# Attention, a max-of-three layer and a leaky layer in split fp32: plain-fp32 pairs, a longer result ring, and Strassen operands made on VectorE alone

## The chip, the cores and the metric

One core of a Trainium2 chip. The metric is the device time of one execution in microseconds (us), lower is better. The engines are named as in the profile: PE (TensorE's matmuls), PEld (its weight loads), DVE (VectorE), ACT (ScalarE), POOL (GpSimd), SP (SyncE, which only issues transfers here).

## What is computed

```python
def _attn_ref(q, k, v, w_phi):            # 4 batches, 8 heads, 576 positions, 64 wide
    def phi(x):
        proj = np.einsum('bhsd,df->bhsf', x, w_phi)          # 128 features
        proj = proj - np.max(np.abs(proj), axis=-1, keepdims=True)
        return np.concatenate([np.exp(proj), np.exp(-proj)], axis=-1)
    q_p, k_p = phi(q), phi(k)
    kv = np.einsum('bhsf,bhsd->bhfd', k_p, v)
    z = np.sum(k_p, axis=2)
    num = np.einsum('bhsf,bhfd->bhsd', q_p, kv)
    den = np.einsum('bhsf,bhf->bhs', q_p, z)[..., None] + 1e-06
    return num / den

def _moe_ref(x, w1, w2, w3, w_out):       # 2304 tokens, 512 -> 768 -> 512
    h = np.maximum(np.maximum(x @ w1, x @ w2), x @ w3)
    return h @ w_out

def _moe2_ref(x, w_in, w_out, alpha):     # 512 -> 2048 -> 512
    h = x @ w_in
    g = np.maximum(h, 0.0) + alpha * np.minimum(h, 0.0)
    return g @ w_out
```

The attention's result goes through the first of the two dense pairs and then through the second. The first pair's weights and the second's come as 64-bit floats and are brought to 32 bits on the chip.

## The kernel before

**Numbers.** Most products are made of split operands: an fp32 tile is written as a high part of type `fp32r` (`hi_act` on ACT or `hi_dve` on DVE) and the rest (`sub`, high part taken from the tile), and a product is three matmuls, high times high, high times low and low times high (`three`). A *plain* product is one matmul of fp32 tiles; the trace records each of those as two instructions.

**The five stages.** (1) Attention, in 16 pairs of heads (`pairs`, 4 per batch). `keys(pair)` projects the keys, takes the largest magnitude of each row, makes both exponentials on ACT and adds keys times values up in one PSUM bank (`kvp`); `queries(pair)` does the same for the queries with a transpose in between, then the numerator and denominator (`num`). The queries of a pair run beside the keys of the next one, at a lower priority. (2) Layer 1 (`layer1`): three products of the attention's result with `w1`, `w2`, `w3` and their maximum, 48 units, of which those of a batch can run once all four pairs of that batch have their result `x`. They fill PE while the later pairs are worked on. (3) Layer 2, `w_out`: 8 chunks of 288 tokens, each with 6 operands `hr` loaded and split by `load_h`, four products, and the results `yo` copied out of PSUM by ACT and stored from ACT's queue. (4) Layer 3, `w_in` with the leaky step. (5) The last layer, by Strassen's scheme: 9 blocks of 256 tokens, each in two halves of the inner dimension; a half has seven products, taken in the order `ORDER = (0, 5, 6, 4, 1, 3, 2)`, each of 12 matmuls. The seven operands `o` of a half are made by `left(block, half)`: two loads `a` (512 KB each), four sums `s1` to `s4` on DVE, and for each operand a high part on ACT and a rest on DVE or POOL. The operands of half 1 have seven places of their own (`op4`); those of half 0 share `ring2`'s 18 places with 14 tiles of the right-hand operand, which stay, so four places turn over.

**Order.** The program is written for a scheduler that puts every engine's instructions in one fixed sequence, by priorities (`tc.high_priority`) and a model of times. Each engine then works its sequence strictly in order: an instruction that waits holds up all that stand behind it on that engine. A tile of a pool can be written again when the last reader of the tile that had its place is done.

**What the change and the steps touch.** `plain` (L146) and `plain_kv` (L149) say which pairs use plain products: batch 0 for the projections, batches 0 and 1 for keys times values; `load_pair`, `features`, `exp_keys` (L206), `keys`, `queries` (L295) follow them. `CONVERT_IN` (L38, L416) says after which pairs the three weight tiles `w123t` of one column block are brought to 32 bits and split: after pairs 0 and 2 to 6. `load_h` (L492) and the loop of layer 2 (L524) hold the buffers of `hr` and `yo`. `left` (L558) makes the last layer's operands.

```python
            for a in range(4):                                       # exp_keys, L215
                A.activation(ev[:, a, 0], pv[:, a], AF.Exp, bias=mx[:, a : a + 1])
                A.activation(ev[:, a, 1], pv[:, a], AF.Exp, bias=my[:, a : a + 1], scale=-1.0)
...
            sub(G if n % 2 and block + half else V, ov[:, 1], src, ov[:, 0])   # left, L578
```

Of the kernel before, what the change touches and what calls it, by code (L numbers as in the profile page):

```python
# [10 lines left out]
F32 = mybir.dt.float32  # L11
# [23 lines left out]
EPS = 1e-6  # L35
XBUFS = (6, 6)
LAG = 1
CONVERT_IN = (0, 2, 3, 4, 5, 6)  # L38
SOON, NOW, LATER, LAST = 400, 1000, -100, -200


# [9 lines left out]
def tile_kernel(ctx: ExitStack, tc: tile.TileContext, qT, kT, tails, v, w_phi, w1, w2, w3, w_out, w_in, w_out2, alpha, out):  # L51
# [92 lines left out]
            raws[pair, what] = t  # L144

    def plain(pair):  # L146
        return pair[0] == 0

    def plain_kv(pair):  # L149
        return pair[0] < 2  # L150
# [55 lines left out]
    def exp_keys(pair):  # L206

        ops = features(pair, "k")
        for g, tiles in enumerate(GROUPS):
            pv, mx = project(ops, tiles)  # L210
            my = ap.tile([P, 4], F32, tag="my", bufs=4, name="my")
            V.tensor_scalar(my, mx, -1.0, None, op0=ALU.mult)
            e = ap.tile([P, 1024], F32, tag="e", bufs=2, name="ke")
            ev = e.rearrange("p (a s f) -> p a s f", s=2, f=P)
# [22 lines left out]
    def keys(pair):  # L237

        rv = raws[pair, "v"]
        if not plain_kv(pair):  # L240
            if not vs:
                vs.extend(ap.tile([P, 5, 3, D], F32R, tag=tag, bufs=1, name=tag) for tag in ("vh", "vl"))
                part = slice(None)
            else:
                part = slice(None, None, 2)
            vh, vl = vs
            hi_act(vh[:, :, part], rv[:, :, part])
            sub(V, vl[:, :, part], rv[:, :, part], vh[:, :, part])
        kvp = bank("kv", 1, "kvp")
        first = True  # L250
        for tiles, e in exp_keys(pair):
            n = len(tiles) * 512
            if plain_kv(pair):
                ops = ((rv, e),)
            else:
                kh = ap.tile([P, 1024], F32R, tag="kh", bufs=2, name="kh")
                kl = ap.tile([P, 1024], F32R, tag="kl", bufs=2, name="kl")
                hi_act(kh[:, :n], e[:, :n])
                sub(V, kl[:, :n], e[:, :n], kh[:, :n])
                ops = ((vh, kh), (vl, kh), (vh, kl))  # L260
            yield
            for i, t in enumerate(tiles):
                for h in range(2):
                    c = slice(i * 512 + h * 256, i * 512 + h * 256 + 256)
                    for x, y in ops:
                        nc.tensor.matmul(
                            kvp[:, h * 256 : h * 256 + 256],
                            x[:, t, h : h + 2].rearrange("p a d -> p (a d)"),
                            y[:, c],
                            start=first,  # L270
                            stop=t == 4 and y is ops[-1][1],
                            skip_group_check=True,
                        )
                        first = False
        yield
        kvs = ap.tile([P, 512], F32, tag="kvs", bufs=1, name="kvs")
        A.activation(kvs, kvp, AF.Copy)
        kvt = bank("kv", 1, "kvt")
        for i in range(4):
            nc.tensor.transpose(kvt[:, i * P : (i + 1) * P], kvs[:, i * P : (i + 1) * P], ident)  # L280
        if plain(pair):
            kvf = ap.tile([P, 2, 2, P], F32, tag=("kvh", "kvl")[pair[1] % 2], bufs=2, name="kvf")
            A.activation(kvf.rearrange("p a b c -> p (a b c)"), kvt, AF.Copy)
            kvs_of[pair] = (kvf,)
            return
# [8 lines left out]

    def queries(pair):  # L295

        parts = ("q",) if plain(pair) else ("qh", "ql")
        qf = []
        for n, (o, w) in enumerate(CHUNKS):
            qf.append([])  # L300
            for x in parts:
                tag = f"qh{n}" if x != "ql" and pair[1] % 2 * len(x) != 1 else f"ql{n}"
                qf[n].append(ap.tile([P, 2, 2, w], F32 if plain(pair) else F32R, tag=tag, bufs=1, name=x))
        nd = [ap.tile([P, S], F32, tag="nd", bufs=3, name="nd") for _ in range(2)]

        def num(n):
            o, w = CHUNKS[n]
            kv = kvs_of[pair]
            for h in range(2):
                pn = bank("p1", 3, "pn") if plain(pair) else bank("pn", 1, "pn")  # L310
                ops = []
                for s in range(2):
                    q_ = [t[:, h, s] for t in qf[n]]
# [7 lines left out]

        for g, tiles, pp in chain(project_queries(pair), tail()):
            o, w = (0, 2 * P, SM)[g], ST if g == 2 else 2 * P
            pt = bank("pt", 1, "pt")
            for i in range(len(tiles)):
                for h in range(2):
                    c = h * len(tiles) * P + i * P
                    nc.tensor.transpose(pt[:, c : c + P], pp[:, 2 * i + h], ident)
            n = min(g, 1)
            dst = [t[:, :, :, o - CHUNKS[n][0] : o - CHUNKS[n][0] + w] for t in qf[n]]  # L330
            if plain(pair):
                e = dst[0]
            else:
                e = ap.tile([P, 2, 2, 256], F32, tag="qe", bufs=2, name="qe")[:, :, :, :w]
            pv = pt[:, : 256 * len(tiles)].rearrange("p (h s) -> p h s", h=2)[:, :, -w:]
            A.activation(e[:, :, 0], pv, AF.Exp)
            A.activation(e[:, :, 1], pv, AF.Exp, scale=-1.0)
            if not plain(pair):
                (hi_dve if g == 1 else hi_act)(dst[0], e)
                sub(V, dst[1], e, dst[0])  # L340
            yield
# [64 lines left out]
    for i, pair in enumerate(pairs):  # L406
        if i + 1 < len(pairs):
            load_pair(pairs[i + 1])
        with tc.high_priority(offset=0 if plain(pair) else SOON if pair[0] == 1 else NOW):
            if pair == (1, 0):  # L410
                hi_dve(wph, wraw)
                sub(V, wpl, wraw, wph)
            run(*([at_priority(LATER, queries(last))] if last else []), keys(pair))
            last = pair
        if i in CONVERT_IN:
            with tc.high_priority(offset=LAST if i < NPAIR - 1 else 0):  # L416
                for j in range(3):
                    run(split_w123(len(w) - (j > 0), j))
        u0 = 3 * (i - NPAIR) - LAG
        for u in range(u0, u0 + 3):  # L420
            if u >= 0:
# [69 lines left out]

    def load_h(c, k):  # L492
        hh, hl = x_tiles(max(c % 2, k // XBUFS[0]))
        pool, tag, bufs = ((xp, "xr", 3), (xp, "xr", 3), (xp, "s1", 2), (gp, "neg", 2))[(2 * c + k) % 4]
        if c == 0:
            pool, tag, bufs = xp, "xr", 3
        hr = pool.tile([P, CH], F32, tag=tag, bufs=bufs, name="hr")
        nc.sync.dma_start(hr, h_d[k, :, c * CH : (c + 1) * CH])
        hi_act(hh, hr)
        sub(V, hl, hr, hh)  # L500
# [23 lines left out]
    for c in range(2 * B):  # L524
# [5 lines left out]
        for m in range(KT):  # L530
# [2 lines left out]
            for k in range(NF1):  # L533
                ops += three(wo[k][:, 0, ms], wo[k][:, 1, ms], *hs[c, k])
            products(p2[m][:, :CH], ops)
            yo = xp.tile([P, CH], F32, tag="ho", bufs=2, name="yo")
            A.activation(yo, p2[m][:, :CH], AF.Copy)
            nc.scalar.dma_start(y_d[m, :, t0 : t0 + CH], yo)
        convert(2)
# [18 lines left out]
    def left(block, half):  # L558

        ready[block, half] = res = {}  # L560
        a = []
        for kh in range(2):
            t = ap4.tile([P, 4, 2 * T], F32, tag="a", bufs=4, name="a")
            r = slice(kh * 8 + half * 4, kh * 8 + half * 4 + 4)
            nc.sync.dma_start(t, g_d[r, :, block * 2 * T : (block + 1) * 2 * T].rearrange("f p n -> p f n"))
            a.append(t)
        (a00, a10), (a01, a11) = ((t[:, :, :T], t[:, :, T:]) for t in a)
        s1, s2, s3, s4 = (ap4.tile([P, 4, T], F32, tag="s", bufs=4, name="s") for _ in range(4))
        V.tensor_tensor(s3, a00, a10, op=ALU.subtract)
        V.tensor_tensor(s1, a10, a11, op=ALU.add)  # L570
        V.tensor_tensor(s2, s1, a00, op=ALU.subtract)
        V.tensor_tensor(s4, a01, s2, op=ALU.subtract)  # L572
        for n, i in enumerate(ORDER):
            src = (a00, a01, s4, a11, s1, s2, s3)[i]
            o = op4.tile([P, 2, 512], F32R, name="o") if half else ring2.tile([P, 2, 512], F32R, tag="w", name="o")
            ov = o.rearrange("p a (f n) -> p a f n", f=4)
            hi_act(ov[:, 0], src)
            sub(G if n % 2 and block + half else V, ov[:, 1], src, ov[:, 0])  # L578
            res[i] = o
            yield  # L580

    V.tensor_scalar(al, al, -1.0, 1.0, op0=ALU.mult, op1=ALU.add)
    load_y(0, 0)
# [129 lines left out]
```

## Time and profile before

| what | value |
|---|---|
| runs of the kernel before | 941.51, 936.77, 939.18 us; median 939.18 |
| the profiled execution | 941.19 us, of which the span of the profile is 939.4 us |
| mean granted clock of TensorE | 0.989 of full speed |
| busy in the span | PE 906.3, DVE 658.9, ACT 487.0, POOL 155.1 us |
| attention beside the first units of layer 1 | about 0 to 377 us |
| layer 2, layer 3, last layer begin | about 466, 547, 750.5 us |

Busy times are shares of engine time; instructions of PE overlap, so the number of matmuls begun in a stretch tells more than its busy time. POOL's 155 us are the 51 rests of the last layer and the issuing of 140 stores.

### The profile page before, as it was taken

The page shows a single profiled execution, that of the slowest core. Times are in us where ns is not written, and L with a number is a line of the kernel's source. Part 1 is how long each engine was busy: PE and PEld are TensorE (multiplying, and loading weights), DVE is VectorE, ACT ScalarE, POOL GpSimd, SP SyncE. Part 2 cuts the span into 40 slices and gives each one's busy share as a digit, 9 for nine tenths or more (in the row PEclk, how much of TensorE's full clock was granted, in tenths as well). Part 3 has the DMA queues.
Part 4 walks back from the last instruction along what each step waited for, and adds up shares of the span by engine and source line. Part 5 has one row for each costly group of instructions (what it writes and reads, how often), then busy time and mean ns, then how long its engine had stood idle before and what let it go on. Part 6 is the DMA issues. An engine that isn't in the chain of part 4 may idle for free.

```text
span 939.4 us, 18181 instructions
## 1 busy us (share of the span) xinstructions
PE 906.3 (96%) x6730; PEld 881.6 (94%) x6730; DVE 658.9 (70%) x1281; ACT 487.0 (52%) x1148; POOL 155.1 (17%) x197
## 2 busy tenths in 40 slices
PE   8778899999999999999999999999999998999998
PEld 6556799999999999999999999999999998999998
DVE  5788866878888752689888575446544588878782
ACT  6667665867667841334356363335333354444441
POOL 0000000000000000001100013333333353444440
PEclk9998899999999999999999999999999999999999
DMA  8455422322233112566676755444643344444421
GB/s 275 142 160 158 131 66 58 101 90 85 79 87 86 33 40 57 190 180 189 198 222 219 246 168 159 152 145 156 206 146 116 113 124 116 154 139 131 135 70 45
DMA packets 83161, 126.01 MB, mean 134 GB/s; under 512 B 14208, under 2 KB 61952, under 8 KB 83072
## 3 DMA queue, kind: packets, MB, share of 16 engines
q1 hardware_dynamic: 71744, 99.47, 35.6%
q0 software_dynamic: 6720, 20.65, 6.1%
q10 hardware_dynamic: 4608, 4.72, 1.5%
q8 instruction: 53, 0.87, 0.4%
q14 instruction: 36, 0.29, 0.1%
HBM read 86.91 MB, written 35.46 MB: 130 GB/s over the span
## 4 chain that ended last, share of the span: by engine, by line
PE 39%; DVE 5%; DMA 5%; ACT 3%; issue 2%; ACTq 0%; DVEq 0%; SPq 0%
PE p L235 23%; PE acc L632 15%; DMA hr<-h_d 2%; DMA st<-in_w_in 2%; DVE o L73 1%; DMA y_d<-yo 1%; DMA st<-in_w_out 1%; ACT xh L67 1%; DVE xl L73 1%; ACT wt L80 1%; DVE s L572 0%; ACT o L67 0%; DVE wt L88 0%; ACT wq L67 0%; DVE wt L86 0%
## 5 line engine op out<-in xcount | busy, mean ns | idle before, releaser
L235 PE MATMUL p<-xh,w123t 128*128 128x288 f32 x1152 | 241.0, 298 | 1.1 <-DVE s L391 0.8
L235 PE MATMUL p<-xh,wi 128*128 128x288 f32 x1024 | 203.7, 296 | 0.0
L235 PEld LDWEIGHTS p<-xh,w123t 128*128 128x128 f32 x1152 | 187.0, 188 | 2.7 <-DVE s L391 1.3
L632 PE MATMUL acc<-wq,o 128*128 128x256 f32 x1512 | 181.7, 282 | 3.2 <-DVE o L73 2.9
L632 PEld LDWEIGHTS acc<-wq,o 128*128 128x128 f32 x1512 | 179.9, 190 | 4.9 <-DVE o L73 4.5
L235 PE MATMUL p<-xl,w123t 128*128 128x288 f32 x576 | 171.6, 298 | 0.0
L235 PEld LDWEIGHTS p<-xh,wi 128*128 128x128 f32 x1024 | 163.2, 188 | 0.0
L235 PE MATMUL p<-xl,wi 128*128 128x288 f32 x512 | 149.5, 293 | 0.0
L603 DVE SCALAR_TENSOR_TENSOR g<-neg,al,p 128x288 f32<-128x288 f32 x128 | 64.3, 512 | 63.6 <-ACT neg L601 59.9
L235 PEld LDWEIGHTS p<-xl,w123t 128*128 128x128 f32 x576 | 108.2, 188 | 0.3
L604 POOL DMA_DIRECT2D g_d<-g x128 | 69.5, 544 | 208.4 <-DVE g L603 204.7
L235 PEld LDWEIGHTS p<-xl,wi 128*128 128x128 f32 x512 | 97.1, 190 | 0.0
L601 ACT ACTIVATE neg<-p 128x288 f32<-128x288 f32 x128 | 51.0, 407 | 86.2 <-PE p L235 81.9
L395 POOL DMA_DIRECT2D h_d<-ho x12 | 7.3, 611 | 466.0 <-DVE ho L393 466.0
L235 PE MATMUL p<-xh,wo 128*128 128x288 f32 x384 | 77.3, 297 | 1.8 <-ACT xh L67 1.8
L67 ACT ACTIVATE o<-s 128x512 fp32r<-128x512 f32 x72 | 44.3, 629 | 54.3 <-PE acc L632 30.0
L73 DVE TENSOR_TENSOR xl<-xr,xh 128x288 fp32r<-128x288 f32 x96 | 42.2, 455 | 37.2 <-ACT xh L67 33.2
L67 ACT ACTIVATE xh<-xr 128x288 fp32r<-128x288 f32 x96 | 41.6, 449 | 47.4 <-DMA xr<-y_d 33.4
L235 PEld LDWEIGHTS p<-xh,wo 128*128 128x128 f32 x384 | 61.2, 188 | 2.5 <-ACT xh L67 2.5
L216 ACT ACTIVATE ke<-pj,mx 128x128 f32<-128x128 f32 x128 | 49.1, 384 | 21.9 <-DVE mx L193 21.6
L193 DVE TENSOR_REDUCE mx<-pj 128x4 f32<-128x512 f32 (+1 forms) x80 | 50.3, 632 | 14.4 <-PE pj L235 14.4
L73 POOL TENSOR_TENSOR o<-s,o 128x512 fp32r<-128x512 f32 x34 | 49.5, 1459 | 64.3 <-ACT o L67 59.4
(133 smaller groups left out, 1695.7 us busy)
## 6 DMA issues: line engine op xcount, KB each, us to landing
g_d<-g POOLq DMA_DIRECT2D x128, 144.0 KB, 2.2
a<-g_d SPq DMA_DIRECT2D x36, 512.0 KB, 3.8
st<-in_w_out SPq DMA_DIRECT2D x22, 512.0 KB, 4.1
wst<-in_w SPq DMA_DIRECT2D x18, 512.0 KB, 4.4
xr<-y_d SPq DMA_DIRECT2D x64, 144.0 KB, 2.4
st<-in_w_in SPq DMA_DIRECT2D x16, 512.0 KB, 3.9
v<-in_v SPq DMA_DIRECT2D x16, 480.0 KB, 3.8
hr<-h_d SPq DMA_DIRECT2D x48, 144.0 KB, 4.2
```

What stands on the lines that cost most here:

```text
L67: A.activation(dst, src, AF.Copy)
L73: eng.tensor_tensor(dst, src, hi.bitcast(F32), op=ALU.subtract)
L80: A.activation(w, high.bitcast(F32), AF.Abs)
L193: V.tensor_reduce(mx, pv, axis=AX.X, op=ALU.max, apply_absolute_value=True, negate=True)
L216: A.activation(ev[:, a, 0], pv[:, a], AF.Exp, bias=mx[:, a : a + 1])
L235: nc.tensor.matmul(dst, x, y, start=i == 0, stop=i == len(ops) - 1, **kw)
L395: (nc.gpsimd if b == B - 1 else nc.sync).dma_start(h_d[f, :, o : o + CH], ho)
L601: A.activation(neg, p, AF.Relu, scale=-1.0)
L603: V.scalar_tensor_tensor(g, neg, al[:, f : f + 1], p, op0=ALU.mult, op1=ALU.add)
L604: nc.gpsimd.dma_start(g_d[f, :, c * CH : (c + 1) * CH], g)
L632: nc.tensor.matmul(acc[i], x, y, start=half == 0 and f == 0 and n == 0 and PLACE[i][1] == 0, stop=half == 1 and f == 3 and n == 2, skip_gr ...
```

## The change

Five things are done at once.

1. `plain` now holds for the first five pairs (batch 0 and pair 0 of batch 1). In batch 1 the `kv` result, the queries' exponentials and `num` follow `plain_kv`, so they too are plain there. `num` of batch 1 takes its bank from `pn` (one) as before and that of batch 0 from `p1` (three); in batch 0 the second transposes of a pair's queries take `pn`'s bank and not `pt`'s.
2. In batch 0 the keys are treated as the queries are: DVE subtracts the largest magnitude into an SBUF tile `pp`, and ACT makes two exponentials of 512 columns out of it where it made eight of 128.
3. The 18 weight tiles `w123t` are converted 2, 1, 2, 1, 3, 3, 3, 3 at a time after pairs 0 to 7, where it was 3 after pairs 0 and 2 to 6.
4. In layer 2 the results `yo` alternate between two pools of two places (they had two in all), and `hr` has the three places of `xr` and the two of `s1` (it also had the two that `yo` now has).
5. In the last layer all rests are made on DVE, each sum is written next to the product that needs it first, and the two loads of a half share one tile of a pool of two where each had its own tile of a pool of four.

```diff
-CONVERT_IN = (0, 2, 3, 4, 5, 6)
+PLAIN = 5
+CONVERT_IN = (2, 1, 2, 1, 3, 3, 3, 3)
     def plain(pair):
-        return pair[0] == 0
+        return pair[0] * NPAIR + pair[1] < PLAIN
...
             pv, mx = project(ops, tiles)
+            e = ap.tile([P, 1024], F32, tag="e", bufs=2, name="ke")
+            ev = e.rearrange("p (a s f) -> p a s f", s=2, f=P)
+            if pair[0] == 0:
+                pp = ap.tile([P, 4, P], F32, tag="pp", bufs=2, name="pp")
+                less_max(pv, mx, pp)
+                A.activation(ev[:, :, 0], pp, AF.Exp)
+                A.activation(ev[:, :, 1], pp, AF.Exp, scale=-1.0)
+                yield tiles, e
+                continue
...
-        if plain(pair):
+        if plain_kv(pair):
             kvf = ap.tile([P, 2, 2, P], F32, tag=("kvh", "kvl")[pair[1] % 2], bufs=2, name="kvf")
...
-                pn = bank("p1", 3, "pn") if plain(pair) else bank("pn", 1, "pn")
+                pn = bank("p1", 3, "pn") if pair[0] == 0 else bank("pn", 1, "pn")
...
-            pt = bank("pt", 1, "pt")
+            pt = bank("pn" if pair[0] == 0 and g == 1 else "pt", 1, "pt")
...
-            if not plain(pair):
+            if not plain_kv(pair):
                 (hi_dve if g == 1 else hi_act)(dst[0], e)
                 sub(V, dst[1], e, dst[0])
...
-        if i in CONVERT_IN:
+        for _ in range(CONVERT_IN[i] if i < len(CONVERT_IN) else 0):
             with tc.high_priority(offset=LAST if i < NPAIR - 1 else 0):
-                for j in range(3):
-                    run(split_w123(len(w) - (j > 0), j))
+                n = sum(len(x) for x in w)
+                run(split_w123(n // 3, n % 3))
...
-        pool, tag, bufs = ((xp, "xr", 3), (xp, "xr", 3), (xp, "s1", 2), (gp, "neg", 2))[(2 * c + k) % 4]
-        if c == 0:
-            pool, tag, bufs = xp, "xr", 3
-        hr = pool.tile([P, CH], F32, tag=tag, bufs=bufs, name="hr")
+        tag, bufs = ("s1", 2) if c and k % 2 else ("xr", 3)
+        hr = xp.tile([P, CH], F32, tag=tag, bufs=bufs, name="hr")
...
-            yo = xp.tile([P, CH], F32, tag="ho", bufs=2, name="yo")
+            pool, tag = ((xp, "ho"), (gp, "neg"))[m % 2]
+            yo = pool.tile([P, CH], F32, tag=tag, bufs=2, name="yo")
...
-        a = []
+        a = ap4.tile([P, 2, 4, 2 * T], F32, tag="a", bufs=2, name="a")
         for kh in range(2):
-            t = ap4.tile([P, 4, 2 * T], F32, tag="a", bufs=4, name="a")
             r = slice(kh * 8 + half * 4, kh * 8 + half * 4 + 4)
-            nc.sync.dma_start(t, g_d[r, :, block * 2 * T : (block + 1) * 2 * T].rearrange("f p n -> p f n"))
-            a.append(t)
+            nc.sync.dma_start(a[:, kh], g_d[r, :, block * 2 * T : (block + 1) * 2 * T].rearrange("f p n -> p f n"))
...
-        V.tensor_tensor(s3, a00, a10, op=ALU.subtract)
-        V.tensor_tensor(s1, a10, a11, op=ALU.add)
-        V.tensor_tensor(s2, s1, a00, op=ALU.subtract)
-        V.tensor_tensor(s4, a01, s2, op=ALU.subtract)
-        for n, i in enumerate(ORDER):
-            src = (a00, a01, s4, a11, s1, s2, s3)[i]
+        def factor(i, src):
             o = op4.tile([P, 2, 512], F32R, name="o") if half else ring2.tile([P, 2, 512], F32R, tag="w", name="o")
             ov = o.rearrange("p a (f n) -> p a f n", f=4)
             hi_act(ov[:, 0], src)
-            sub(G if n % 2 and block + half else V, ov[:, 1], src, ov[:, 0])
+            sub(V, ov[:, 1], src, ov[:, 0])
             res[i] = o
-            yield
+
+        factor(0, a00)
+        V.tensor_tensor(s1, a10, a11, op=ALU.add)
+        V.tensor_tensor(s2, s1, a00, op=ALU.subtract)
+        yield
+        factor(5, s2)
+        V.tensor_tensor(s3, a00, a10, op=ALU.subtract)
+        yield
+        factor(6, s3)
+        yield
+        factor(4, s1)
+        yield
+        factor(1, a01)
+        yield
+        factor(3, a11)
+        V.tensor_tensor(s4, a01, s2, op=ALU.subtract)
+        yield
+        factor(2, s4)
```

**ACT's sequence at the first pair.** `ke` is the exponentials of one group of keys, `pj` the projections in PSUM, `mx` and `my` minus and plus the largest magnitude. Before:

```order
L216 ACTIVATE ke_120<-pj_113,mx_116 128x128
L217 ACTIVATE ke_120<-pj_113,my_118 128x128
L216 ACTIVATE ke_120<-pj_113,mx_116 128x128
L217 ACTIVATE ke_120<-pj_113,my_118 128x128
L216 ACTIVATE ke_120<-pj_113,mx_116 128x128
L217 ACTIVATE ke_120<-pj_113,my_118 128x128
L216 ACTIVATE ke_120<-pj_113,mx_116 128x128
L217 ACTIVATE ke_120<-pj_113,my_118 128x128
L216 ACTIVATE ke_140<-pj_133,mx_136 128x128
```

Now:

```order
L217 ACTIVATE ke_118<-pp_119 128x4x128
L218 ACTIVATE ke_118<-pp_119 128x4x128
L217 ACTIVATE ke_132<-pp_133 128x4x128
L218 ACTIVATE ke_132<-pp_133 128x4x128
L233 ACTIVATE ke_147<-ppt_141,signs_84 128x2x128 x2
```

Eight exponentials of a group have become two, and they read the SBUF tile `pp`, so the PSUM bank `pj` is free once DVE has made `pp`.

**DVE's sequence at the turn from one block of the last layer to the next.** Before, `o_10627` and `o_10633` are two of the last three rests of a block's half 0 (the one between them is on POOL), `s_10861` and `s_10863` are sums of its half 1, and `a_10992` is the first load of the next block's half 0:

```order
L644 TENSOR_TENSOR out0_10723<-acc_10485,u2_10721 128x256
L73 TENSOR_TENSOR o_10769<-s_10746,o_10769 128x512
L73 TENSOR_TENSOR o_10627<-a_10605,o_10627 128x512
L571 TENSOR_TENSOR s_10861<-s_10860,a_10856 128x512
L73 TENSOR_TENSOR o_10633<-s_10610,o_10633 128x512
L572 TENSOR_TENSOR s_10863<-a_10858,s_10861 128x512
L73 TENSOR_TENSOR o_10868<-a_10856,o_10868 128x512
L73 TENSOR_TENSOR o_10874<-s_10862,o_10874 128x512
L569 TENSOR_TENSOR s_10998<-a_10992 128x512
```

Now, with `o_10676`, `o_10679`, `o_10683` the last three rests of half 0 of the fifth block, `a_10654` its tile of loads and `a_10905` the sixth block's:

```order
L662 TENSOR_TENSOR out0_10773<-acc_10537,u2_10771 128x256
L74 TENSOR_TENSOR o_10818<-s_10795,o_10818 128x512
L74 TENSOR_TENSOR o_10676<-a_10654,o_10676 128x512
L74 TENSOR_TENSOR o_10679<-a_10654,o_10679 128x512
L583 TENSOR_TENSOR s_10908<-a_10905 128x512
L74 TENSOR_TENSOR o_10683<-s_10660,o_10683 128x512
L584 TENSOR_TENSOR s_10909<-s_10908,a_10905 128x512
L587 TENSOR_TENSOR s_10910<-a_10905 128x512
```

The next block's first sum `s_10908` now stands ahead of this block's last rest `o_10683`. It stands so at four turns, into the sixth, seventh, eighth and ninth block; at the earlier ones the last rest stands ahead of what reads the next load. The matmuls of these four blocks stand in the order of the products.

## Rows read from the trace of the kernel before

**Rows 1.** The page's part 1: busy time, share, instructions.

```profile
PE 906.3 (96%) x6730; PEld 881.6 (94%) x6730; DVE 658.9 (70%) x1281; ACT 487.0 (52%) x1148; POOL 155.1 (17%) x197
```

**Rows 2.** Windows of 25 us: length, busy time (instructions) by engine, granted clock, DMA.

```profile
75.00:100.00 25.00, 21.89 (x119) 19.07 (x117) 20.25 (x49) 19.82 (x52) 0.00 (x0) 0.86 0.50 145
...
125.00:150.00 25.00, 25.00 (x183) 24.47 (x182) 16.05 (x37) 13.88 (x38) 0.00 (x0) 1.00 0.20 57
```

**Rows 3.** PE's waits, whole span: us in total, times, longest.

```profile
PE pt L328 <- ACT q L337: 6.0, 3, 3.4
PE pj L235 <- ACT ke L217: 3.2, 2, 2.9
```

**Rows 4.** Groups by shape, 0 to 300 us: count, busy us, mean ns, idle before.

```profile
L336 ACT ACTIVATE qe<-pt 128x512 f32<-128x512 f32 x19 | 11.8, 623 | 3.1 <-PE pt L328 3.1
...
L197 DVE TENSOR_TENSOR pp<-pj,mx 128x512 f32<-128x512 f32 x28 | 19.1, 682 | 0.0
```

**Rows 5.** Timeline of ACT at the first keys: start, length.

```profile
7.15 0.36 ACT L217 ACTIVATE ke<-pj,my 128x128 f32<-128x128 f32 x1
7.40 0.37 ACT L216 ACTIVATE ke<-pj,mx 128x128 f32<-128x128 f32 x1
```

**Rows 6.** Timeline of PE: split and plain products back to back.

```profile
85.86 1.89 PE L235 MATMUL pn<-q,kvf 128*128 128x256 f32 x8
87.59 0.38 PE L328 MATMUL pt<-ident,ppt 128*128 128x128 f32 x2
...
155.08 0.28 PE L235 MATMUL pj<-wph,xhq 128*128 128x256 f32 x1
155.20 0.28 PE L235 MATMUL pj<-wpl,xhq 128*128 128x256 f32 x1
```

**Rows 7.** Windows in layer 2, and one at its end.

```profile
480.00:490.00 10.00, 9.09 (x67) 8.64 (x66) 7.86 (x17) 6.91 (x17) 0.00 (x0) 1.00 0.74 231
500.00:530.00 30.00, 28.06 (x203) 26.70 (x202) 24.26 (x51) 16.23 (x39) 0.00 (x0) 1.00 0.79 252
540.00:560.00 20.00, 20.00 (x154) 20.00 (x153) 15.20 (x34) 12.88 (x31) 3.24 (x5) 1.00 0.56 172
```

**Rows 8.** Waits of ACT, whole span.

```profile
ACT yo L537 <- DMA y_d<-yo: 15.9, 11, 4.3
...
ACT xh L67 <- DMA hr<-h_d: 10.2, 7, 3.0
```

**Rows 9.** Timeline of PE, start of the last layer.

```profile
750.50 27.26 PE L632 MATMUL acc<-wq,o 128*128 128x256 f32 x226
780.61 19.63 PE L632 MATMUL acc<-wq,o 128*128 128x256 f32 x152 [2.85 <-DVE o L73]
```

**Rows 10.** Timelines of DVE and POOL, start of the last layer.

```profile
755.99 1.38 DVE L73 TENSOR_TENSOR o<-s,o 128x512 fp32r<-128x512 f32 x1 [0.35 <-ACT o L67]
...
760.73 0.68 DVE L569 TENSOR_TENSOR s<-a 128x512 f32<-128x512 f32 x1
761.33 0.68 DVE L73 TENSOR_TENSOR o<-s,o 128x512 fp32r<-128x512 f32 x1
...
777.33 1.08 DVE L569 TENSOR_TENSOR s<-a 128x512 f32<-128x512 f32 x1
...
755.53 3.01 POOL L73 TENSOR_TENSOR o<-s,o 128x512 fp32r<-128x512 f32 x2 [3.04 <-ACT o L67]
```

**Rows 11.** Last layer: one window, ACT at a block's start, loads `a` issued and landed.

```profile
840.00:860.00 20.00, 19.96 (x170) 19.76 (x170) 16.43 (x24) 9.06 (x16) 9.27 (x7) 1.00 0.43 130
...
856.92 0.63 ACT L67 ACTIVATE o<-a 128x512 fp32r<-128x512 f32 x1 [0.83 <-PE acc L632]
858.35 0.63 ACT L67 ACTIVATE o<-a 128x512 fp32r<-128x512 f32 x1 [0.80 <-PE acc L632]
...
754.92 1.12 SPq L565 DMA_DIRECT2D a<-g_d  x2
...
DMA to landing us min/median/max: 3.7/3.8/5.0
```

More of the change, by code (lines that the diff above doesn't have):

```diff
@@ L210, in exp_keys @@
             pv, mx = project(ops, tiles)
+            e = ap.tile([P, 1024], F32, tag="e", bufs=2, name="ke")
[7 more added lines that the diff above has]
+                continue
             my = ap.tile([P, 4], F32, tag="my", bufs=4, name="my")
             V.tensor_scalar(my, mx, -1.0, None, op0=ALU.mult)
-            e = ap.tile([P, 1024], F32, tag="e", bufs=2, name="ke")
-            ev = e.rearrange("p (a s f) -> p a s f", s=2, f=P)
             for a in range(4):
@@ L295, in queries @@
     def queries(pair):
-        parts = ("q",) if plain(pair) else ("qh", "ql")
+        parts = ("q",) if plain_kv(pair) else ("qh", "ql")
         qf = []
@@ L302, in queries @@
                 tag = f"qh{n}" if x != "ql" and pair[1] % 2 * len(x) != 1 else f"ql{n}"
-                qf[n].append(ap.tile([P, 2, 2, w], F32 if plain(pair) else F32R, tag=tag, bufs=1, name=x))
+                qf[n].append(ap.tile([P, 2, 2, w], F32 if plain_kv(pair) else F32R, tag=tag, bufs=1, name=x))
         nd = [ap.tile([P, S], F32, tag="nd", bufs=3, name="nd") for _ in range(2)]
@@ L330, in queries @@
             dst = [t[:, :, :, o - CHUNKS[n][0] : o - CHUNKS[n][0] + w] for t in qf[n]]
-            if plain(pair):
+            if plain_kv(pair):
                 e = dst[0]
@@ L408, in tile_kernel @@
             load_pair(pairs[i + 1])
-        with tc.high_priority(offset=0 if plain(pair) else SOON if pair[0] == 1 else NOW):
-            if pair == (1, 0):
+        with tc.high_priority(offset=(0, SOON, NOW, NOW)[pair[0]]):
+            if i == PLAIN - 1:
                 hi_dve(wph, wraw)
@@ L560, in left @@
         ready[block, half] = res = {}
-        a = []
+        a = ap4.tile([P, 2, 4, 2 * T], F32, tag="a", bufs=2, name="a")
         for kh in range(2):
-            t = ap4.tile([P, 4, 2 * T], F32, tag="a", bufs=4, name="a")
             r = slice(kh * 8 + half * 4, kh * 8 + half * 4 + 4)
-            nc.sync.dma_start(t, g_d[r, :, block * 2 * T : (block + 1) * 2 * T].rearrange("f p n -> p f n"))
-            a.append(t)
-        (a00, a10), (a01, a11) = ((t[:, :, :T], t[:, :, T:]) for t in a)
+            nc.sync.dma_start(a[:, kh], g_d[r, :, block * 2 * T : (block + 1) * 2 * T].rearrange("f p n -> p f n"))
+        (a00, a10), (a01, a11) = ((a[:, kh, :, :T], a[:, kh, :, T:]) for kh in range(2))
         s1, s2, s3, s4 = (ap4.tile([P, 4, T], F32, tag="s", bufs=4, name="s") for _ in range(4))
-        V.tensor_tensor(s3, a00, a10, op=ALU.subtract)
-        V.tensor_tensor(s1, a10, a11, op=ALU.add)
-        V.tensor_tensor(s2, s1, a00, op=ALU.subtract)
-        V.tensor_tensor(s4, a01, s2, op=ALU.subtract)
-        for n, i in enumerate(ORDER):
-            src = (a00, a01, s4, a11, s1, s2, s3)[i]
+        def factor(i, src):
             o = op4.tile([P, 2, 512], F32R, name="o") if half else ring2.tile([P, 2, 512], F32R, tag="w", name="o")
```

## The prediction

> **What bounds the kernel now.** I read the page's busy times first, then windows along the span, PE's waits, and the timelines of the stages that the change touches. PE is busy for 96% of the span [rows 1], so the time is PE's work plus the stretches in which it starves, and a saving on another engine counts only there. In the windows, from 125 us on PE is busy in all of its 25 us with 183 matmuls; before that it is not: from 75 to 100 us it begins 119, is busy 21.9 of 25 us, and its granted clock averages 0.86, while DVE is busy 20.25 and ACT 19.8 us [rows 2]. So up to about 110 us DVE and ACT set the pace together, and after that PE does, except in two places. In layer 2, 67 matmuls begin from 480 to 490 us and 203 from 500 to 530 us, where an undisturbed window has 154 in 20 us, 0.130 us each [rows 7]: 10 and 28 too few, 4.9 us. At the start of the last layer PE stands for 2.85 us waiting for an operand's rest on DVE [rows 9]. From 840 to 860 us it starts 170 matmuls and is busy 19.96 of 20 us [rows 11]: there is nothing left to gain there, but something to lose.
>
> **Attention: what is taken off ACT.** In batch 0, 64 exponentials of 128 columns go, which start 0.25 us apart [rows 5], 16.0 us of ACT; 16 of 512 columns come, 0.62 us each [rows 4], 9.9 us: ACT is 6.1 us shorter. DVE gets 8 subtractions of 0.68 us [rows 4], 5.4 us; they lie on the same path, between projection and exponential. In PE's waits, 6.0 us go to transposes that wait for the bank `pt` until ACT has read it, and 3.2 us to projections that wait for a bank until ACT has made the exponentials out of it [rows 3]. The first gets a second bank; the second now waits for DVE's subtraction only. The gain lies between 0 (DVE, which gets more, sets the pace alone) and 9.2 us (both waits gone). I take 6 us, what ACT loses, since the bank that PE waits for is ACT's to give back. The splits that batch 1 drops on DVE and ACT I cost at nothing: they lie mostly after 110 us, where PE's own work covers them. Moving weight conversions to later pairs I cost at nothing too; they are fillers at a low priority, and the last of them, for the sixth column block, stands one pair later, ahead of the unit that needs it.
>
> **Attention: what PE pays.** Batch 1's products become plain: 27 projections (pair 0 of batch 1), 48 numerators of 256 and 48 of 320 columns go, as split matmuls; 9 plain projections and 16 and 16 plain numerators come. Split ones of 256 columns start 0.12 us apart; four plain ones (eight recorded) take 1.73 us, 0.43 each [rows 6]. By columns, 320 cost 0.15 and 0.54. Gone: 75 x 0.12 + 48 x 0.15 = 16.2; new: 25 x 0.43 + 16 x 0.54 = 19.4. PE gets 3.2 us more, and since this falls where it is full, all of it counts.
>
> **Layer 2.** ACT waits 15.9 us in 11 places for a `yo` to be stored before it can copy the next, and 10.2 us for `hr` [rows 8]. Behind a waiting copy stand the high parts of the next chunk, for which PE starves. Four places for `yo` remove the first wait; `hr` loses two places of seven, so late in a chunk its sixth load waits for the second to be split. The ends are 0 and the whole 4.9 us; I take 3.5, near the whole, since the removed wait is the larger one.
>
> **The start of the last layer.** DVE's operations with two SBUF inputs take 0.68 us undisturbed, and start 0.60 us apart; beside POOL's rests they take longer [rows 10]. Nine such, the first at 755.99 us with 1.38 and the last at 777.33 us with 1.08, take 13.9 us together (1.54 each) instead of 9 x 0.68 = 6.1: 7.8 us lost. POOL's nine rests of that stretch, about 1.5 us each there [rows 10], come to DVE at 0.60, 5.4 us. DVE is 2.4 us earlier, which takes that much off the 2.85 us. After the stop 152 matmuls take 19.63 us; at the 0.1206 us of the 226 before it (27.26 us) they would take 18.3 [rows 9], so the slower stretch after the stop costs 1.3 us, and goes with it. Together 3.7 us, between 0 and 4.15.
>
> **The running last layer.** In each block DVE now has 22 operations of 0.60 and 7 of half that width (0.34 us, an estimate from 0.68), 15.6 of the block's 19.8 us (168 matmuls at the pace of [rows 11]); this fits. What does not is a load that has come under a shared tile. Take a block's start as 0. Its fifth and sixth operands get their high parts on ACT at 1.4 and 2.85 us, when the first two products give their places back (856.92 and 858.35 us for a block that starts at 855.5) [rows 11]. The sixth's rest ends at 2.85 + 0.65 + 0.68 = 4.2 us, and it is the last reader of the tile `a`. Only then can both loads for the next block go out; before, each load had its own tile, and the first could go as soon as the sums were made. A load lands 3.8 us after its issue at the median and 5.0 at most; two issues that went out within 1.12 us of each other are among these [rows 11]. So the second lands at 8.4 to 9.6 us. In four blocks the next block's first sum, which reads both loads, stands in DVE's sequence ahead of the seventh operand's rest: this one is ready after 0.68 + 0.60 us, at 9.7 to 10.9. PE comes to the seventh product at 6 x 1.41 = 8.5 us and, after two matmuls on the high part, needs the rest at 8.7. It waits 1.0 to 2.2 us, four times. I take 1.6, the middle, as two loads together are nearer to the maximum but nothing else is on the queues: +6.4 us. If DVE also falls behind in the earlier blocks (15.6 us of work behind a load of 4.2 to 5.4 us is 19.8 to 21.0 for a block of 19.8, less one or two rests made meanwhile), the first of the four waits takes some 4 us more; the upper end is +11.
>
> The Trainium skill, DMA: Bandwidth & Descriptors, section Bandwidth, gives 6.15 us of transfer for 1 MB against the 3.8 us that the trace shows for one of these half-megabyte loads alone. As an estimate by that page, two loads together would land some 1.3 us later than I took, and the sum below would be 5 us higher; no run here has shown two issued back to back.
>
> **The sum.** -6 + 3.2 - 3.5 - 3.7 + 6.4 = -3.6 us. The profiled execution took 941.2 us, so 937.6 on its scale; it lies 2.0 us above the median of the runs, 939.2. Forecast for the median: **935.6 us**, 0.4% less. About 0.5%, 4.7 us, is what a measurement of this kernel can tell from no change.
>
> **Rivals** (all on the median's scale).
> - *The gains come whole and the loads come soon.* Both bank waits, all of layer 2's and the whole stop go, and PE waits 1.0 us in four blocks: -9.2 + 3.2 - 4.9 - 4.15 + 4.0 = -11.1, 928.1 us. For it: DVE keeps 19% of its time free before 110 us. Against: DVE's new work stands on the path. Chance 0.25.
> - *The last layer's loads decide, slower than before.* The first sum holds up the seventh rest for over 2 us, DVE drifts, and each stop lowers the clock as the one at 780 us did: +11 + 4 x 1.3 = +16.2 in place of +6.4, so +6.2, 945.4 us. It decides from a landing of about 5 us for the pair. For it: the maximum in the trace is from two loads near each other. Against: small stops in layer 2 left the granted clock at 1.00 [rows 7]. Chance 0.15.
> - *Attention gains nothing.* DVE sets the pace alone and PE still pays: +2.4, 941.6 us. For it: DVE is the busier of the two in the window [rows 2]. Chance 0.18.
> - *Layer 2 does not do what is said:* five places for `hr` starve PE as `yo` did: -0.1, 939.1 us. Chance 0.06.
>
> **How the numbers follow.** My sum has 0.36; its own range is 931 to 940, of which I give 0.16 to below 934.5 and 0.20 to above. Faster: 0.16 + 0.25 = 0.41. Slower: 0.15 + 0.02 from the upper side of the third rival. Same: 0.42. The range 926 to 946 takes in both outer cases and leaves out about 2 in 10 beyond them.
>
> **What would show it.** Right: in PE's waits the rows of `pt` and of `pj` behind ACT shrink; the row of `yo` behind its store goes; no stop near 778 us; and in blocks five to eight one wait each for DVE's `o`, 1 to 2 us, at the seventh product, with DVE idle until a load lands. Wrong: PE full through the last layer, matmuls from 25 to 110 us no denser than now, or ACT waiting for `hr` where it waited for `yo`.

## The result, and the profile after

The changed kernel takes **925.83 us** at the median of 6 runs (923.4 to 928.34), the kernel before 939.74 us in the same comparison: a ratio of 0.9855, 95% interval 0.9829 to 0.9882, 13.9 us less. The forecast was 935.6 us; the measured median lies 0.2 us under the range's lower end. The sign was right, the size was not: the sum had -3.6 us. The nearest case was the rival in which the gains come whole (928.1 us).

The changed kernel's profiled execution has a span of 926.4 us, 13.0 us under that of before (939.4). The page's part 1, which answers to [rows 1]:

```profile
PE 900.7 (97%) x6689; PEld 877.8 (95%) x6689; DVE 643.2 (69%) x1306; ACT 471.6 (51%) x1092; POOL 77.3 (8%) x146
```

The first matmul of each stage in the two timelines says where the 13.0 us are:

| stage | begins before, after | length before, after | difference |
|---|---|---|---|
| attention and layer 1, to layer 2's start | 0, 0 | 465.8, 462.1 | -3.7 |
| layer 2 | 465.8, 462.1 | 81.2, 78.0 | -3.2 |
| layer 3 | 547.0, 540.1 | 203.5, 204.4 | +0.9 |
| last layer, PE | 750.5, 744.5 | 184.9, 177.8 | -7.1 |

The prediction had -2.8, -3.5, 0 and +2.7 for these. The first three look well met, and the last is off by ten. The runs below show that the layer 2 row is not what it seems either. Nor is the whole first row the change's: runs 1 to 3 leave PE's, ACT's and DVE's sequences as they were up to layer 3, and in their traces layer 2 begins at 463.0, 463.4 and 464.0 us. Layer 3's 0.9 us was not looked into.

PE's timeline of the changed kernel's last layer is one row, where [rows 9] had two with a stop between them:

```profile
744.53 177.82 PE L650 MATMUL acc<-wq,o 128*128 128x256 f32 x1512
```

All 1512 matmuls follow one another at 0.1176 us. There is neither a stop near 778 us nor any of the four waits that the prediction put at the seventh products.

PE's waits, longest first (us in total, times, longest), to set beside [rows 3]:

```profile
PE pj L243 <- ACT ke L225: 4.8, 1, 4.8
PE kvp L274 <- ACT kvf L291: 3.1, 2, 2.5
PE pj L243 <- DVE dc L359: 2.8, 1, 2.8
PE pt L336 <- ACT q L345: 2.5, 3, 1.2
```

The 6.0 us of transposes behind `q` are 2.5, and the projections' wait for the keys' exponentials of batch 0 is gone (L225 is the exponential of the later batches' keys, still 128 columns at a time). ACT's waits in layer 2, beside [rows 8]:

```profile
ACT xh L68 <- DMA hr<-h_d: 18.2, 14, 2.7
ACT yo L544 <- PE p L243: 6.4, 7, 2.0
```

No `yo` waits for a store any more, but the wait for `hr` has grown from 10.2 to 18.2 us. The prediction had named this as a sign that it would be wrong there.

### The profile page after: what moved, and what is told of

Same layout as the page of the kernel before. It is cut to its first block, busy times and chain, and to the rows that moved or that the text cites. A ratio compares the mean times of both kernels' runs of the same rounds, so it can differ in the third digit from the quotient of the medians.

```text
span 926.4 us, 17946 instructions
## 1 busy us (share of the span) xinstructions
PE 900.7 (97%) x6689; PEld 877.8 (95%) x6689; DVE 643.2 (69%) x1306; ACT 471.6 (51%) x1092; POOL 77.3 (8%) x146
## 4 chain that ended last, share of the span: by engine, by line
PE 27%; issue 19%; POOL 4%; DMA 2%; DVE 1%; ACT 0%; POOLq 0%; DVEq 0%; SPq 0%; ACTq 0%
PE acc L650 19%; PE p L243 8%; POOL g_d L622 4%; DMA st<-in_w_in 1%; DMA a<-g_d 1%; DMA xr<-y_d 0%; POOL h_d L403 0%; DVE wt L89 0%; DVE xl L74 0%; DMA g_d<-g 0%; DVE wt L87 0%; ACT wt L81 0%; DVE ho L401 0%; DVE wt L85 0%; POOLq L622 0%
## 5 line engine op out<-in xcount | busy, mean ns | idle before, releaser
L650 PE MATMUL acc<-wq,o 128*128 128x256 f32 x1512 | 177.8, 280 | 0.0
L650 PEld LDWEIGHTS acc<-wq,o 128*128 128x128 f32 x1512 | 177.7, 188 | 0.0
L243 PE MATMUL p<-xl,wo 128*128 128x288 f32 x192 | 56.1, 292 | 1.0 <-DVE xl L74 1.0
L68 ACT ACTIVATE o<-a 128x512 fp32r<-128x512 f32 x54 | 33.8, 630 | 37.0 <-PE acc L650 28.6
L81 ACT ACTIVATE wt<-st 128x512 f32<-128x512 f32 x38 | 25.6, 673 | 48.6 <-DMA st<-in_w_in 26.4
```

The lines of the kernel that those rows point to most:

```text
L68: A.activation(dst, src, AF.Copy)
L81: A.activation(w, high.bitcast(F32), AF.Abs)
L243: nc.tensor.matmul(dst, x, y, start=i == 0, stop=i == len(ops) - 1, **kw)
L650: nc.tensor.matmul(acc[i], x, y, start=half == 0 and f == 0 and n == 0 and PLACE[i][1] == 0, stop=half == 1 and f == 3 and n == 2, skip_gr ...
```

## Experiments: the parts alone

Each run is compared with the kernel before, in the same job; a ratio of 0.001 is 0.94 us.

**1. The new last layer alone.** The whole of `left` as changed, in the kernel before.

> The kernel before with the whole new last layer (rests on DVE, sums next to their products, one tile for both loads) and nothing else. From the two traces the last layer went from 185.0 us to 177.8 us. Theory: that gain belongs to the last layer's code, so this run is 7 us faster than before (ratio 0.9925, 0.991 to 0.994) and PE has no stop in its last 178 us. Rival: the stop near 778 us in the kernel before came from how layer 3 handed over, and part of the 7 us needs the other parts of the change: then 0 to 4 us faster, with a stop left at the start of the last layer.

Measured: 0.9942 (0.9917 to 0.9967), 5.4 us faster. PE's last layer takes 177.8 us without a stop. The gain belongs to the last layer's own code. What in it?

**2. Only the rests moved.**

```diff
-            sub(G if n % 2 and block + half else V, ov[:, 1], src, ov[:, 0])
+            sub(V, ov[:, 1], src, ov[:, 0])
```

> The kernel before with the rests of the last layer on DVE in place of every other one on GpSimd; sums in front and four load tiles as before. Theory (GpSimd slows DVE): DVE's operations of two SBUF inputs take 0.68 us everywhere in the last layer, the 3 us stop and the 0.2 us stops once a block go, 6 to 7 us faster (ratio 0.9925 to 0.9936). Rival (the place of the sums): DVE has 51 rests more behind four sums in a row and is later, PE keeps its stops: same or up to 5 us slower.

Measured: 0.993 (0.9904 to 0.9956), 6.6 us faster. Here are the groups of DVE in the last layer (751 to 935 us of the kernel before; count, busy us, mean ns, idle before):

```profile
L73 DVE TENSOR_TENSOR o<-a,o 128x512 fp32r<-128x512 f32 x36 | 35.8, 995 | 8.7 <-ACT o L67 8.6
L73 DVE TENSOR_TENSOR o<-s,o 128x512 fp32r<-128x512 f32 x35 | 30.7, 877 | 21.3 <-ACT o L67 21.2
L569 DVE TENSOR_TENSOR s<-a 128x512 f32<-128x512 f32 x16 | 17.9, 1120 | 0.6
L570 DVE TENSOR_TENSOR s<-a 128x512 f32<-128x512 f32 x16 | 16.4, 1026 | 0.0
L572 DVE TENSOR_TENSOR s<-a,s 128x512 f32<-128x512 f32 x17 | 13.5, 795 | 0.5
L571 DVE TENSOR_TENSOR s<-s,a 128x512 f32<-128x512 f32 x16 | 10.9, 679 | 0.1
```

and in this run (746 to 930 us):

```profile
L73 DVE TENSOR_TENSOR o<-s,o 128x512 fp32r<-128x512 f32 x69 | 46.8, 687 | 18.2 <-ACT o L67 18.0
L73 DVE TENSOR_TENSOR o<-a,o 128x512 fp32r<-128x512 f32 x53 | 36.2, 684 | 5.6 <-ACT o L67 5.6
L572 DVE TENSOR_TENSOR s<-a,s 128x512 f32<-128x512 f32 x17 | 11.7, 688 | 0.3
L569 DVE TENSOR_TENSOR s<-a 128x512 f32<-128x512 f32 x16 | 11.0, 687 | 0.2
L570 DVE TENSOR_TENSOR s<-a 128x512 f32<-128x512 f32 x16 | 11.0, 686 | 0.2
L571 DVE TENSOR_TENSOR s<-s,a 128x512 f32<-128x512 f32 x16 | 10.9, 684 | 0.1
```

Add up the columns: before, 136 operations take 125.2 us, 0.92 each; now 187 take 127.6 us, 0.68 each. DVE took over 51 operations at the price of 2.4 us in 178. GpSimd had relieved DVE of almost nothing, and 42 of DVE's 136 operations had taken over 0.8 us. PE has no stop left:

```profile
745.43 177.92 PE L632 MATMUL acc<-wq,o 128*128 128x256 f32 x1512
```

**3. Only the sums moved.** Each sum stands next to the product that needs it, the rests stay divided.

```diff
-        V.tensor_tensor(s3, a00, a10, op=ALU.subtract)
...
             res[i] = o
+            if n == 0:
+                V.tensor_tensor(s1, a10, a11, op=ALU.add)
+                V.tensor_tensor(s2, s1, a00, op=ALU.subtract)
...
```

> The kernel before with each sum of the last layer next to the product that needs it, and the rests divided between DVE and GpSimd as before. Theory (GpSimd slows DVE): the operations beside GpSimd's stay at 1.1 to 1.8 us, and PE keeps most of its stops: within 2 us of before (ratio 0.998 to 1.002). Rival (the place of the sums): the stops go, 5 to 7 us faster (0.9925 to 0.9947).

Measured: 1.0011 (0.9991 to 1.0031). The stops stay, as PE's timeline shows:

```profile
746.03 25.63 PE L635 MATMUL acc<-wq,o 128*128 128x256 f32 x216
772.83 1.73 PE L635 MATMUL acc<-wq,o 128*128 128x256 f32 x10 [1.16 <-ACT o L67]
776.39 20.39 PE L635 MATMUL acc<-wq,o 128*128 128x256 f32 x160 [1.84 <-DVE o L73]
797.03 133.54 PE L635 MATMUL acc<-wq,o 128*128 128x256 f32 x1126 [0.24 <-DVE o L73]
```

So the place of the sums is worth nothing by itself, and the last layer's gain is GpSimd's absence. GpSimd's own rests, about 1.5 us each, could have been late for PE too; but the stop of before ended on a rest of DVE [rows 9], and PE's waits in that last layer name none of GpSimd's.

**4. Loads that really come late.** In the changed kernel, each half's loads get a place of their own.

```diff
-        a = ap4.tile([P, 2, 4, 2 * T], F32, tag="a", bufs=2, name="a")
+        a = ap4.tile([P, 2, 4, 2 * T], F32, tag=f"a{half}", bufs=1, name="a")
```

> The changed kernel with one place for the loads of half 0 and one for those of half 1, in place of two places that the halves share. In the changed kernel's trace the loads for the next half 0 go out 0.1 us into a block, into the place that half 1 gave back; here they can only go out when half 0's sixth rest is done, 4.4 us into the block, as the prediction had it for the change. Theory (the prediction's mechanism is real, its time of issue was wrong): the loads land 4 us later, and where the next first sum stands ahead of a last rest PE waits 1 to 3 us; 2 to 12 us slower than the changed kernel (928 to 938). Rival: PE does not need these loads before the block's end, and where the sequence puts the rest first nothing waits: 925 to 927 us, no stop in the last layer.

Measured: 0.9866 (0.9839 to 0.9893), 924.6 us, the changed kernel's time. The loads do go out late; SP's issues and PE's last layer in this run:

```profile
830.38 5.13 SPq L571 DMA_DIRECT2D a<-g_d  x4
...
849.74 0.38 SPq L571 DMA_DIRECT2D a<-g_d  x1
```

```profile
743.13 179.82 PE L650 MATMUL acc<-wq,o 128*128 128x256 f32 x1512
```

In the block that begins at 822.2 us the first load for the next one goes out 8.2 us in, in the block of 842.3 us 7.4 us in. PE's last layer is 2.0 us longer than the changed kernel's, and not 4 to 11 us. It loses them in two places, at 824.2 and from 883.2 to 885.5 us, 2 to 4 us behind the landing of a block's last load (820.57 and 881.36 us). DVE's sequence had been made anew with the other places and mostly has the last rests ahead of the sums, so this bounds what late loads cost, not what they would cost in the changed kernel's sequence. That one can't be had with late loads, since the places set both.

**5. Layer 2's buffers alone** (`load_h` and `yo` as in the change).

> The kernel before with only the buffers of layer 2 changed (four places for yo, five for hr). Theory: layer 2 took 81.1 us before and 78.0 us after, and that is this part's: 3.1 us faster (ratio 0.9967, 0.995 to 0.998), no wait of ACT for a yo's store. Rival (five places for hr starve PE as the stores did, and the after kernel's layer 2 was better by its later start): within 1 us.

Measured: 1.0019 (1.0003 to 1.0034), 1.8 us **slower**. Windows and PE's wait in layer 2 of this run:

```profile
470.00:480.00 10.00, 7.56 (x52) 7.12 (x52) 8.07 (x18) 4.29 (x11) 0.54 (x1) 0.93 0.70 215
480.00:490.00 10.00, 9.87 (x58) 9.52 (x57) 10.00 (x22) 8.16 (x19) 0.00 (x0) 0.73 0.80 248
```

```profile
PE p L235 <- ACT xh L67: 2.4, 1, 2.4
```

The stops between 500 and 530 us are gone (77 or 78 matmuls in each 10 us), but one of 2.4 us has come at 476, where a high part waits for an `hr`, and after it the granted clock is 0.73: 20 matmuls missing in 10 us. In this execution `hr` lost what `yo` got.

**6. Batch 0's keys through `pp` and the second bank for the transposes**, in the kernel before.

> The kernel before with batch 0's keys through pp (two exponentials of 512 columns a group) and the second transposes in pn's bank; weight conversions and batch 1 as before. Theory of the prediction: 6 us faster (0 to 9.2), ratio 0.9936, layer 2 beginning at 460 us in place of 465.8. Rival (DVE, which gets 8 subtractions more, sets the pace alone): within 2 us.

Measured: 0.993 (0.9909 to 0.995), 6.6 us faster. The first 125 us of the kernel before, and then of this run (PE, PEld, DVE, ACT, POOL; the third number from the end is the granted clock):

```profile
0.00:125.00 125.00, 103.09 (x502) 84.06 (x503) 96.68 (x213) 86.60 (x230) 0.70 (x6) 0.93 0.53 167
0.00:125.00 125.00, 105.16 (x554) 87.87 (x555) 101.74 (x221) 80.92 (x191) 0.70 (x6) 0.99 0.54 171
```

ACT is busy for 5.7 us less and PE begins 52 matmuls more. The granted clock is higher too, 0.99 against 0.93, so part of the 52 may be the clock's. In runs 1 to 3, with the sequence of before, PE begins 516 to 526 at 0.93 to 0.95.

**7. The keys alone**, without the second bank.

> The kernel before with batch 0's keys through pp (two exponentials of 512 columns a group), without the second bank for the transposes. Theory of the prediction: the two waits are separate (3.2 us of projections behind the keys' exponentials, 6.0 us of transposes behind the queries'), ACT's 6.1 us come from the keys alone, and most of the 6.6 us that both gave together is here: 4 to 6 us faster (ratio 0.9936 to 0.9957). Rival: the second bank is what counts, and this alone gives under 2 us (over 0.998).

Measured: 0.9935 (0.9917 to 0.9954), 6.1 us faster. PE's first waits in this run:

```profile
PE pj L242 <- DVE pp L197: 5.2, 2, 4.3
PE kvt L287 <- ACT kvs L284: 3.4, 2, 1.7
...
PE pt L335 <- ACT qe L344: 1.8, 1, 1.8
```

The 6.0 us of transposes that wait for `q` (L337 of before) have nearly gone without a second bank for them, and a wait for DVE's `pp` of 5.2 us stands there instead. Waits of this kind are handed on from one bank to another. The run does not part the two things that the keys' new form does: it shortens ACT's work, and it frees the bank `pj` once DVE has made `pp`. A run with `pp` and eight exponentials would have parted them.

**8. Plain products in batch 1 alone.**

> The kernel before with plain products in batch 1 as in the change, and nothing else. Theory of the prediction: PE gets 3.2 us more work and nothing else changes, 3.2 us slower (ratio 1.0034). Rival: the splits that go from DVE and ACT (19.6 us of DVE by the counts) are worth as much where both are still behind, and it comes out within 1 us or faster by up to 4 us.

Measured: 0.9997 (0.9978 to 1.0016): nothing. Two windows of this run, 25 us each, DVE being the third pair of numbers:

```profile
100.00:125.00 25.00, 23.42 (x155) 21.77 (x156) 16.96 (x39) 14.68 (x41) 0.00 (x0) 1.00 0.31 96
125.00:150.00 25.00, 25.00 (x158) 23.09 (x157) 10.81 (x30) 14.21 (x43) 0.00 (x0) 1.00 0.24 68
```

In the kernel before, the first of these windows reads:

```profile
100.00:125.00 25.00, 22.12 (x131) 20.27 (x131) 22.88 (x47) 16.27 (x42) 0.00 (x0) 0.86 0.38 124
```

DVE drops from 22.88 to 16.96 us and PE begins 155 in place of 131, some of them plain ones, which are dearer; from 125 us on it begins 158 in place of 183 [rows 2]. It looks as if PE were given time at one place and paid it back at the next. But the 131 come with a granted clock of 0.86, and runs 1 to 3, whose sequence is the same there, begin 149, 153 and 144 in that window. DVE's relief is real (runs 1 to 3 have 22.0 to 22.4 us); how much of it reaches PE is not shown.

**9. The conversions spread alone.**

> The kernel before with the 18 weight conversions spread 2, 1, 2, 1, 3, 3, 3, 3 after pairs 0 to 7, and nothing else. Theory of the prediction: nothing, within 1 us. Rival: fewer conversions among the first pairs let the first results come earlier (or the first units of layer 1 later): 1 to 4 us either way.

Measured: 0.9993 (0.9975 to 1.0011): nothing, as forecast.

## Experiments: parts taken out of the changed kernel, and put together

**10. Batch 1 split again.**

> The changed kernel with batch 1's products split as before (only batch 0 plain). Theory: the 3.2 us of PE work that the prediction charged to plain products cost nothing in the kernel before, where PE waited for ACT and DVE there, but cost their price in the changed kernel, where the keys' exponentials no longer hold PE up: 3 us faster than the changed kernel (ratio to before 0.982 in place of 0.9855). Rival: the 123 split matmuls' operands bring back as much waiting for DVE as PE gains: 0.985 to 0.987.

Measured: 0.9871 (0.9849 to 0.9892), 927.2 us. Not faster than the changed kernel, but its trace does not settle the charge: layer 2 begins at 458.9 us, 3.2 us earlier than in the changed kernel's, and then takes 83.3 us in place of 78.0, with one wait of 3.9 us for a high part of `hr`. Run 12 is the better comparison.

**11. Layer 2's old buffers.**

> The changed kernel with layer 2's buffers as before (two places for yo, seven for hr). Theory of the prediction: 3 us slower than the changed kernel (ratio to before 0.9887). Rival, from the run that had this part alone and was 0.2% slower: the places that hr loses cost as much as those that yo gains, and this is within 1.5 us of the changed kernel or faster (0.984 to 0.987).

Measured: 0.9843 (0.9824 to 0.9863), 924.83 us. The changed kernel is no slower without its new buffers. Together with run 5 this takes layer 2's term away.

**12. The three pieces that gave something**, in the kernel before: the keys, the second bank, the new last layer.

> The kernel before with the three pieces that gave something alone: batch 0's keys through pp, the second bank for the transposes, and the new last layer. Batch 1, the weight conversions and layer 2's buffers as before. If the pieces add up: 0.993 x 0.9935 = 0.9866, 926 us; if plain products cost 3 us in the changed kernel and its ring gives nothing, this is the faster one of the two: 0.982 to 0.985. If the ring or the plain products do carry part of the changed kernel's gain: 0.987 to 0.99.

Measured: 0.9853 (0.9834 to 0.9872), 925.19 us. That is the whole of the change (0.9855). The two gains multiply: 0.993 x 0.9942 = 0.987 from runs 6 and 1, 0.993 x 0.993 = 0.986 from runs 6 and 2. No version beats the changed kernel by more than the intervals. Run 11 differs from this one in the plain products of batch 1 and the spread conversions alone: 924.83 and 925.19 us, with layer 2 beginning at 458.5 and 458.4 us. So the 3.2 us do not show in the changed kernel either.

## Why the prediction was right in sign and wrong in size

| step | predicted, us | measured, us | by run |
|---|---|---|---|
| ACT's relief in attention | -6 (0 to -9.2) | -6.6 (-8.5 to -4.7) | 6 |
| plain products on PE | +3.2 | -0.3 (-2.1 to +1.5) | 8 (and 11 against 12) |
| conversions | 0 | -0.7 (-2.3 to +1.0) | 9 |
| layer 2 | -3.5 (0 to -4.9) | +1.8 (+0.3 to +3.2) | 5 (and 11) |
| last layer, start and running | -3.7 + 6.4 = +2.7 | -5.4 (-7.8 to -3.1) | 1 |

**ACT's relief was right in its size; its reason is not shown.** ACT's saved 6.1 us came as 6.1 us (run 7), but the interval is 4.3 to 7.8 us, and so close a match is luck. The runs do not part ACT's shorter work from the earlier release of `pj`, nor from the granted clock. The second bank, which the prediction counted into the upper bound, is not seen in the times: 0.5 us between runs 6 and 7, inside both intervals, which could hide 2 us.

**The failed step is "The running last layer", +6.4.** By the two traces the running layer gained 1.9 us in place of costing 6.4, and the start gained 5.1 in place of 3.7. The prediction took the loads of the next block to wait for "the last reader of the tile", half 0's sixth rest at 4.2 us. The mechanism exists, but it governs another pair of loads. Here is the changed kernel's block that begins at 843.3 us, DVE first and then SP's issues:

```profile
842.72 0.69 DVE L74 TENSOR_TENSOR o<-a,o 128x512 fp32r<-128x512 f32 x1 [0.24 <-ACT o L68]
...
847.02 0.69 DVE L74 TENSOR_TENSOR o<-a,o 128x512 fp32r<-128x512 f32 x1 [0.74 <-ACT o L68]
849.44 0.69 DVE L583 TENSOR_TENSOR s<-a 128x512 f32<-128x512 f32 x1 [1.73 <-DMA a<-g_d]
850.05 0.68 DVE L74 TENSOR_TENSOR o<-s,o 128x512 fp32r<-128x512 f32 x1
...
855.01 0.69 DVE L583 TENSOR_TENSOR s<-a 128x512 f32<-128x512 f32 x1 [0.67 <-DMA a<-g_d]
```

```profile
843.44 0.92 SPq L571 DMA_DIRECT2D a<-g_d  x2
...
847.74 16.36 SPq L571 DMA_DIRECT2D a<-g_d  x4
```

The sixth rest of half 0 ends at 847.71, 4.4 us into the block, as computed, and two loads go out at 847.74 and 848.16 (the row puts them together with the next block's two). But the sum at 849.44, the one that stands ahead of the last rest, can't read those 1.7 us later. It reads the pair of 843.44, whose second load landed at 849.35 and which went out when half **1**'s sixth rest (842.72) was done. Half 1's operands are made up to a block ahead; their rests stand above half 0's in the very rows of DVE's sequence that were shown (`o_10818` above `o_10679`), so their place came free first and the next tile took it. The prediction had taken the places to go round by turns. The sum then runs 6.1 us into the block and the last rest ends at 7.4, where PE needs it at 8.7: DVE waits there for the load, PE does not.

The transfer itself was slower than the prediction took: two back to back take 843.44 to 849.35, 5.9 us, where the sum had 4.2 to 5.4 and one alone takes 3.8. The Trainium skill, DMA: Bandwidth & Descriptors, section Bandwidth, gives 6.15 us for 1 MB, for a transfer that GpSimd issues. The trace's 5.9 us, from the first issue on SP to the second landing, lies near that figure. It did not decide, because the issue was 4 us earlier than the sum had it.

**"There is nothing left to gain there" was wrong too.** The row of 840 to 860 us [rows 11] was read as full because PE is busy for 19.96 of 20 us. Finer windows of the kernel before, at the same turn (a window counts every matmul that touches it, so only differences tell):

```profile
839.50:840.50 1.00, 1.00 (x11) 1.00 1.01 369
840.50:841.50 1.00, 0.96 (x8) 1.00 0.60 219
```

Three matmuls fewer touch the second window than the first, and the two steps from matmul to matmul around 841.3 us are 0.3 us longer together than at the steady pace. The same place shows at 800.9, 821.0, 861.1, 881.1 and 901.1 us: 1.9 us in six turns. DVE and GpSimd there:

```profile
839.49 1.78 DVE L73 TENSOR_TENSOR o<-a,o 128x512 fp32r<-128x512 f32 x1
841.20 0.68 DVE L571 TENSOR_TENSOR s<-s,a 128x512 f32<-128x512 f32 x1
```

```profile
839.02 1.70 POOL L73 TENSOR_TENSOR o<-a,o 128x512 fp32r<-128x512 f32 x1 [2.38 <-ACT o L67]
```

DVE's rest starts at 839.49 and ends at 841.27, 0.55 us after GpSimd's operation: as if it had done its 0.68 us of work almost wholly behind it, and PE's gap ends at 841.33. The Trainium skill, SBUF — State Buffer, section SBUF: two separate sides, says that an operation of DVE with two inputs in SBUF and one of GpSimd that reads SBUF exclude each other for a whole instruction; this row agrees. The prediction used that effect at the stop of 778 us and not in the blocks after it, where the same rows were to be had.

**The start was undersized** (the sum had 3.7): 3.0 us of stop instead of 2.85, 0.5 us of stutter just ahead of it, and more for the clock. The window behind the stop:

```profile
780.50:785.50 5.00, 4.89 (x28) 0.66 0.73 212
785.50:790.50 5.00, 5.00 (x45) 1.00 0.15 52
```

28 in place of 45 matmuls at 0.1176 us are 2.0 us, where the sum had 1.3. 3.0 + 0.5 + 1.6 for the clock without the stop's own edge + 1.9 for the turns = 7.0, the last layer's 7.1.

**Layer 2 was read off one execution.** Run 2 has the kernel before's sequence unchanged up to the last layer on PE, ACT and DVE, and yet its layer 2 reads, beside [rows 7]:

```profile
480.00:490.00 10.00, 10.00 (x78) 10.00 (x77) 9.55 (x20) 7.69 (x19) 0.00 (x0) 1.00 0.63 200
500.00:530.00 30.00, 29.03 (x211) 27.87 (x210) 21.34 (x45) 15.55 (x38) 0.00 (x0) 1.00 0.76 252
```

In place of 10 and 28 missing matmuls, none and some 20: its layer 2 takes 78.5 us, about what the changed kernel's does. Four executions of this sequence (before and runs 1 to 3) take 81.2, 80.0, 78.5 and 78.5 us, and PE waits there for high parts of `hr` for 1.8, 1.4, 0.5 and 0.3 us: the profiled execution of before was a poor one. The new buffers have good and poor executions too, 78.0 us in the changed kernel and run 4, 82.2 and 83.3 in runs 5 and 10. The rival "Layer 2 does not do what is said", which had 0.06, is what happened to this term, and the run with this part alone is slightly slower.

**The plain products' charge** is not seen in run 8, nor in run 11 against run 12. The likely step is "The splits that batch 1 drops on DVE and ACT I cost at nothing": the kernel before's window from 100 to 125 us, shown at run 8, has DVE busy for 22.88 us and PE below its later pace, so that stretch was not covered by PE's work. That these splits make up for just 3.2 us is argued and not shown.

## What to carry to other kernels

Before giving GpSimd half of an elementwise job, add up DVE's time with and without it: here 51 operations on GpSimd cost DVE as much time as doing them itself. A window in which PE is "busy" 99.8% can still lose 1.5%: compare the matmuls in fine windows with the same count at an undisturbed pace. And read which place a load goes to from what is released first in the engine's sequence, and a small stall from more than one execution, before charging either.

## What was not expected of the hardware

After the 3 us stop, PE runs about ten matmuls from 780.61 us on at the full pace and only then, from 782.0 to 785.4 us, 16 of them at 0.213 us each, with a granted clock of 0.50, the lower of its two levels; the drop comes 1.4 us after the work resumes. In run 5 a stop of 2.4 us was followed by a clock of 0.73 in the next 10 us, while the stops in layer 2 of before, at most 1.0 us, left it at 1.00 [rows 7].
